# Attention and a rational feed-forward on one core: half-unit sums moved to accumulating DMAs, copies moved from ScalarE to VectorE, all steps reordered

## The chip, the cores and the metric

The kernel runs on one core of a Trainium2 chip. The metric is the device time of one execution in microseconds (us). The runs of the kernel before took 218.06, 218.3 and 219.33 us; their median is 218.3 us.

The core has a matrix engine (TensorE, PE in the profile, with its weight loads as PEld), VectorE (DVE), ScalarE (ACT), GpSimd (POOL) and SyncE (SP). Each engine runs its own instructions strictly in the order in which they were issued to it; an instruction that waits holds up everything behind it on that engine. Loads and stores are DMAs: here SP and ACT issue plain ones (the profile's queues q1 and q10), and POOL issues those that change the type or add to what lies at the target (queue q0). All of them run on the core's 16 DMA engines.

## What is computed

```python
# gated linear attention: 4 batches, 8 heads, 768 steps, head size 48
f = 1.0 / (1.0 + np.exp(-f_logit))
for t in range(S):
    state = f[:, :, t, :, None] * state + np.einsum('bhd,bhe->bhde', k[:, :, t], v[:, :, t])
    y[:, :, t] = np.einsum('bhd,bhde->bhe', q[:, :, t], state)
# feed-forward with a rational activation: 3072 tokens, 384 -> 2048 -> 384; x is y, tokens by heads
h = x @ w_in
P = a[0] + a[1]*h + a[2]*h**2 + a[3]*h**3
Q = 1.0 + abs(b[0])*abs(h) + abs(b[1])*h**2
out = (P / (Q + 1e-06)) @ w_out
```

## The kernel before

**Units.** The work is cut into 12 units (numbered 0 to 11; unit n is chunk n // 4 of batch n % 4) of 256 tokens. A unit passes through an attention part and a feed-forward part. In the feed-forward part the 2048 hidden columns are 16 blocks of 128; a step that takes "8 16" works on blocks 8 to 15, a half unit of 128 partitions x 2048 elements; quarters have four blocks.

**The order.** Nothing schedules the instructions automatically. A string, `ORDER`, lists 861 steps; the program issues them one by one, so this list fixes the order on each engine and each queue. `@n` names one of four PSUM slots of two banks each; a slot is used again only when the last reader of what it held is done. `ld 2 f >mk.0.1` means that this load may not begin before the step `mk 0 1` is done.

**Steps of the attention part**, with their engine: `ld n f/k/q` loads (SP), `ld n v` load (POOL, with a change of type); `ef`, `ls` exp and log of the gate (ACT); `cs` cumulative sums over time by a triangular matrix (PE); `A` their exp (ACT); `xa` products of q and k with them (DVE); `T` transposes (PE) and `Te` their copy out of PSUM (ACT with `s`, else DVE); `sc` scores (PE), `mk` their mask (DVE); `vm` a copy of parts of v (POOL); `yi`, `yb` the output y (PE); `ye` its scaled copy into the feed-forward's input xT (ACT); `kv`, `si` the new state in PSUM (PE); `ae` a small exp (ACT); `st` the state's scaled copy (DVE).

**Steps of the feed-forward part:** `h` (or its halves `ha`, `hb`) the first product (PE); `hy` its copy to bf16 (ACT); `sq` h squared (DVE; `sa` on ACT); `ab` |h| into the tile z (DVE). Then z + h2 is formed in one of three ways: `u` by two matmuls with the identity, followed by `ln` (ACT); `zd` by a DMA that adds h2 to z in memory, or `zv` by DVE, both followed by `lz` (ACT). `ex` is the exp that makes 1/Q out of that log (ACT). `p1`, `p2`, `pm` form the parts of P (DVE); `ta` (a DMA that adds) or `tv` (DVE) forms their sum, the tile gall; `gm` multiplies it by 1/Q (DVE); `o` is the second product (PE), `oe` its copy out of PSUM, `so` the store (SP, the last on ACT).

**At the start** `cz`, `cu`, `ci`, `cm` make constants, `wi` and `wo` load the two weight matrices in four parts each (POOL), `ab_` loads the coefficients a and b, `fa` works out scales from b (nine tiny DVE instructions), `fr` reads two of them into ACT registers, `fb` scales a, and `dz k` issues k matmuls whose result is not used.

The three ways of a sum, as the code has them:

```python
def zd(n, m0, m1):
    nc.gpsimd.dma_start(out=fl(s["z"], m0, m1), in_=fl(s["h2"], m0, m1), accum_op=ALU.add)
def ta(n, m0, m1):
    nc.gpsimd.dma_start(out=fl(s["g"], m0, m1), in_=fl(s["hy"], m0, m1), accum_op=ALU.add)
def tv(n, m0, m1):
    return nc.vector.tensor_add(fl(s["g"], m0, m1), fl(s["g"], m0, m1), fl(s["hy"], m0, m1))
```

## Time and profile before

| | value |
|---|---|
| median of 3 runs | 218.3 us (218.06 to 219.33) |
| span of the profiled execution | 216.3 us, 2.0 us under that median |
| instructions | 7159 |
| DMA traffic | 42.13 MB in 60910 packets |
| `zd` and `ta` DMAs | 18 and 17 |
| `tv` and `zv` on DVE | 9 and 2 |
| granted TensorE clock | 1.000 |

The span runs from the first to the last instruction that the profile shows. "Busy" is the time in which an engine has an instruction under way; for PE the ends of the matmuls are modelled. A row of the profile by line gives the line of the kernel, engine, operation, the tiles written and read, the count, then busy us and the mean duration of one. Line numbers are those of the kernel before; in the changed kernel they are one to five less.

### The profile page before, as it was taken

To read this page: it belongs to the slowest core of one execution; us is meant where nothing else is said; L and a number is where in the kernel's file an instruction comes from. 1 tells how busy PE (TensorE), PEld (TensorE's weight loads), DVE (VectorE), ACT (ScalarE), POOL (GpSimd) and SP (SyncE) were. 2 spreads that over 40 slices of the span, in tenths; PEclk is the share of its full clock that TensorE was granted. 3 is DMA by queue.
4 is the path that set the end of the run, shared out by engine and by line. 5 is a ranking of instruction groups with operands and counts; after the bars stand their busy time and mean duration, and the time that the engine had idled before them with its cause. 6 is when DMAs were issued, how large, how long until landed. Compare 5 with 4: busy or idle time off the path is not lost.

```text
span 216.3 us, 7159 instructions
## 1 busy us (share of the span) xinstructions
PE 203.2 (94%) x3166; PEld 140.1 (65%) x3166; DVE 202.7 (94%) x246; ACT 200.8 (93%) x211; POOL 81.6 (38%) x91
## 2 busy tenths in 40 slices
PE   6989989699799999999999999999999999999993
PEld 2457658468377657658758658668668678676551
DVE  3588999999999999999999999999999999999991
ACT  4746899999999999999999999999999999999991
POOL 5250247120157803014954205954232516433300
PEclk9999999999999999999999999999999999999999
DMA  5999999999598999958999997999889793999863
GB/s 132 248 226 194 243 212 226 207 221 250 136 246 143 231 237 271 149 101 195 197 232 216 211 251 179 173 234 222 160 159 228 142 162 70 170 194 188 154 234 145
DMA packets 60910, 42.13 MB, mean 195 GB/s; under 512 B 51152, under 2 KB 54992, under 8 KB 60880
## 3 DMA queue, kind: packets, MB, share of 16 engines
q0 software_dynamic: 21232, 22.81, 66.0%
q1 hardware_dynamic: 39360, 18.68, 33.7%
q8 instruction: 24, 0.39, 0.7%
q10 hardware_dynamic: 288, 0.20, 0.3%
q14 instruction: 6, 0.05, 0.1%
HBM read 25.17 MB, written 4.72 MB: 138 GB/s over the span
## 4 chain that ended last, share of the span: by engine, by line
ACT 42%; DVE 21%; PE 18%; DMA 8%; issue 6%; POOL 3%; POOLq 0%; ACTq 0%; DVEq 0%
ACT qi L530 11%; ACT hy L488 10%; PE op L570 9%; ACT lq L526 8%; DMA fn<-in_f_logit_dram 4%; DMA z<-h 4%; PE warm L302 3%; DVE gall L548 3%; ACT A L309 3%; DVE scm L360 3%; DVE qkp L315 3%; PE hp L458 2%; DVE gall L560 2%; DVE gall L556 2%; ACT qkT L337 2%
## 5 line engine op out<-in xcount | busy, mean ns | idle before, releaser
L570 PE MATMUL op<-w_out_sb,gall 128*128 128x384 bf16 x384 | 70.1, 326 | 0.4 <-ACT hy L488 0.4
L458 PE MATMUL hp<-xT,w_in_sb 128*128 128x256 bf16 x564 | 65.3, 272 | 1.3 <-ACT xT L439 1.1
L458 PEld LDWEIGHTS <-w_in_sb 128*128 128x128 bf16 x564 | 55.0, 98 | 11.0 <-issue 2.8
L570 PEld LDWEIGHTS <-gall 128*128 128x128 bf16 x384 | 35.5, 98 | 23.6 <-DVE gall L560 0.9
L488 ACT CAST hy<-hp 128x1024 bf16<-128x1024 f32 x48 | 47.4, 1073 | 1.7 <-PE hp L482 1.2
L530 ACT ACTIVATE qi<-lq 128x2048 bf16<-128x2048 f32 (+1 forms) x26 | 46.9, 1845 | 0.0
L367 POOL COPY vmp<-vn 128x128 bf16<-128x128 bf16 x24 | 33.7, 1417 | 32.1 <-DMA vn<-in_v_dram 18.9
L526 ACT ACTIVATE lq<-z 128x2048 f32<-128x2048 bf16 (+1 forms) x20 | 36.9, 1846 | 0.6 <-DMA z<-h 0.5
L552 POOL DMA_DIRECT2D gall<-hy x17 | 14.8, 926 | 50.7 <-ACT A L309 11.5
L522 POOL DMA_DIRECT2D z<-h x18 | 17.3, 1065 | 36.3 <-issue 10.5
L560 DVE TENSOR_TENSOR gall<-gall,qi 128x2048 bf16<-128x2048 bf16 (+1 forms) x26 | 29.6, 1143 | 0.3 <-ACT qi L530 0.2
L548 DVE TENSOR_TENSOR gall<-gall,h 128x2048 bf16<-128x2048 bf16 (+1 forms) x26 | 29.4, 1138 | 0.0
L492 DVE TENSOR_TENSOR h<-hy 128x2048 bf16<-128x2048 bf16 (+1 forms) x26 | 27.3, 1059 | 1.5 <-ACT hy L488 1.4
L360 DVE TENSOR_TENSOR scm<-sc,mask 128x1024 bf16<-128x1024 f32 x24 | 28.4, 1211 | 0.0
L309 ACT ACTIVATE A<-cs 128x768 f32<-128x768 f32 (+1 forms) x26 | 19.6, 816 | 0.0
L500 DVE TENSOR_SCALAR z<-hy 128x2048 uint16<-128x2048 uint16 (+1 forms) x28 | 17.1, 618 | 0.1
L534 DVE TENSOR_SCALAR gall<-hy,a_sb 128x4096 bf16<-128x4096 bf16 (+1 forms) x14 | 16.9, 1210 | 0.2 <-ACT hy L488 0.2
L539 DVE TENSOR_SCALAR hy<-hy,a_sb 128x4096 bf16<-128x4096 bf16 (+1 forms) x14 | 16.6, 1184 | 0.0
L200 POOL DMA_DIRECT2D vn<-in_v_dram x12 | 13.2, 1104 | 2.2 <-PE y L374 2.2
L315 DVE TENSOR_TENSOR qkp<-kn,A 128x768 bf16<-128x768 f32 (+1 forms) x13 | 11.5, 887 | 2.0 <-ACT A L309 2.0
L278 ACT ACTIVATE fn<-fn 128x768 f32<-128x768 f32 (+1 forms) x13 | 10.7, 825 | 2.8 <-DMA fn<-in_f_logit_dram 2.7
L337 ACT COPY qkT<-tp 128x1024 f32<-128x1024 f32 (+1 forms) x12 | 12.5, 1041 | 0.7 <-PE tp L327 0.7
(72 smaller groups left out, 262.2 us busy)
## 6 DMA issues: line engine op xcount, KB each, us to landing
gall<-hy POOLq DMA_DIRECT2D x16, 512.0 KB, 6.7
z<-h POOLq DMA_DIRECT2D x15, 512.0 KB, 7.4
fn<-in_f_logit_dram SPq DMA_DIRECT2D x11, 384.0 KB, 7.4
kn<-in_k_dram SPq DMA_DIRECT2D x11, 384.0 KB, 9.8
qn<-in_q_dram SPq DMA_DIRECT2D x11, 384.0 KB, 7.2
out_dram<-osb SPq DMA_DIRECT2D x11, 384.0 KB, 4.1
vn<-in_v_dram POOLq DMA_DIRECT2D x12, 192.0 KB, 8.0
w_in_sb<-in_moe_w_in_dram POOLq DMA_DIRECT2D x4, 384.0 KB, 8.2
```

Of the source, the lines that this page charges most:

```text
L309: nc.scalar.activation(t, src, AF.Exp, scale=1.0 if x else -1.0)
L315: return nc.vector.tensor_mul(s["qk"][:, :, x, hh, 0:D], s["qk"[x]][:, hh].rearrange("p h i d -> p i h d"), A_sb[:, :, x].rearrange("p i ( ...
L360: return nc.vector.tensor_mul(t, s["sc", g].rearrange("s r a i t -> s (r a) (i t)"), mb)
L367: nc.gpsimd.tensor_copy(s["vm"][:, :, :, 32 * x:32 * x + 16], src)
L458: nc.tensor.matmul(t[:, m - m0, :], w_in_sb[:, kk, m * P:(m + 1) * P], s["x"][:, kk].rearrange("p i j t -> p (i j t)"), start=(kk == 0), s ...
L488: nc.scalar.copy(fl(big(s, "hy", "hy", 3), m0, m1), fl(s["hp", m0], 0, m1 - m0))
L492: return nc.vector.tensor_mul(fl(big(s, "h2", "h2", 2), m0, m1), fl(s["hy"], m0, m1), fl(s["hy"], m0, m1))
L526: nc.scalar.activation(fl(lq, m0, m1), fl(s["z"], m0, m1), AF.Ln, scale=regs[2], bias=1.0 + 1e-6)
L530: nc.scalar.activation(fl(qi, m0, m1), fl(lq, m0, m1), AF.Exp, scale=-1.0)
L548: return nc.vector.tensor_mul(fl(s["g"], m0, m1), fl(s["g"], m0, m1), fl(s["h2"], m0, m1))
L560: return nc.vector.tensor_mul(fl(s["g"], m0, m1), fl(s["g"], m0, m1), fl(qi, m0, m1))
L570: nc.tensor.matmul(s["op", j][:, j, 0:DM], s["g"][:, m, P * j:P * j + P], w_out_sb[:, m, :], start=(s["on", j] == 1), stop=(s["on", j] == KF))
```

## The change

Two step functions get a choice of engine (`hy` gets one too, which the new order does not use):

```diff
     def ye(n, *args):
-        k0, k1 = [x for x in args if x != "s"] or (0, KD)
+        k0, k1 = [x for x in args if x not in ("s", "v")] or (0, KD)
...
-        return nc.scalar.mul(s["x"][:, k0:k1].rearrange("p k i j t -> p j (k i) t"),
-                             s["y"][:, :, k0 * C:k1 * C].rearrange("p j (k t) -> p j k t", t=R), regs[0])
+        dst = s["x"][:, k0:k1].rearrange("p k i j t -> p j (k i) t")
+        src = s["y"][:, :, k0 * C:k1 * C].rearrange("p j (k t) -> p j k t", t=R)
+        if "v" in args:
+            return nc.vector.tensor_scalar(dst, src, sig[:, 0:1], None, op0=ALU.mult)
+        return nc.scalar.mul(dst, src, regs[0])
```

In the list of steps, which has 861 entries again, these differ in kind:

- `ye` of units 2, 3 and 6 goes from ACT to DVE, and so does `Te` of unit 5.
- `tv` becomes `ta` for the halves 0 0 8, 1 0 8, 1 8 16, 2 8 16, 3 8 16 and the quarters 11 8 12 and 11 12 16; `ta 11 0 4` becomes `tv`. That is 23 accumulating DMAs on gall where there were 17, and 3 sums on DVE where there were 9.
- `zd 3 8 16`, `zd 5 8 16` and `zd 11 0 4` become `zv`; `zv 4 8 16` and `zv 6 0 8` become `zd`. That is 17 and 3 where there were 18 and 2.

Every other step stands in the list as often as before, with the same blocks; their places and slots are all new. The start, before:

```
ld 0 f 2 4; cz 0; ab_ b a; cu 0; cz 1; ld 0 f 0 2; ld 1 f; ci; cu 1; ld 0 v; ld 0 k 0 2; ld 0 k 2 4; fa
ld 0 q 2 4; ef 0 2 4; ls 0 2 4; cm; ef 0 0 2; dz 9 @2; cs 0 2 4 @2; fr; cz 3; ls 0 0 2; ld 0 q 0 2; ab_ a s
ld 1 k; dz 5 @3; cs 0 0 2 @3; ef 1; ld 1 q; ls 1; vm 0 1; A 0 1 0 2; wi 12 16 >ls.1; dz 4 @0; cs 1 @0
A 0 1 2 4; xa 0 1 0 2; A 0 0 2 4; wi 8 12; cz 2; A 0 0 0 2; xa 0 1 2 4; dz 3 @1; kv 0 @2; wi 4 8
xa 0 0 0 2; si 0 0; ae 0; dz 1 @1; T 0 0 2 @1; wi 0 4; xa 0 0 2 4; st 0 0; Te 0 0 2 s; T 0 2 4 @3; A 1 1
ld 1 v; Te 0 2 4; A 1 0; vm 0 0; sc 0 0 @1; si 0 1; mk 0 0; sc 0 1 @3; mk 0 1; ld 2 f >mk.0.1; ld 2 k
ld 3 f; yi 0 1 @0; yb 0 0 2; ye 0 0 1 s; xa 1 1; dz 2 @1; yb 0 2 4; ye 0 1 3 s; st 0 1; dz 1 @3
ha 0 12 16 @3; hb 0 12 16; xa 1 0; fb; hy 0 12 16; h 0 8 12 @1; sq 0 12 16; T 1 @3; hy 0 8 12; ab 0 12 16
u 0 12 16 @2; Te 1 s; sq 0 8 12; h 0 4 8 @1; p1 0 8 16; ln 0 12 16; ld 4 f; ab 0 8 12; pm 0 8 16
u 0 8 12 @2; hy 0 4 8; p2 0 8 16; ln 0 8 12; dz 1 @3; sc 1 1 @1; sc 1 0 @3; sq 0 4 8; h 0 0 4 @0; ef 2
```

and in the changed kernel:

```
ld 0 f 2 4; cu 0; cz 1; ld 0 f 0 2; cz 0; ld 1 f; cu 1; dz 5 @3; ld 0 k 2 4; ld 0 q 2 4; ld 0 v; cm; ld 0 q 0 2
dz 9 @0; ld 0 k 0 2; cz 2; ci; ld 1 k; ld 1 q; ef 0 2 4; ab_ a s; ab_ b a; ef 0 0 2; ls 0 0 2; ls 0 2 4
cs 0 0 2 @3; ef 1; cs 0 2 4 @1; ls 1; fa; A 0 0 0 2; vm 0 0; A 0 0 2 4; ld 1 v; A 0 1 0 2; A 0 1 2 4; dz 1 @3
wi 4 8; fr; xa 0 0 2 4; dz 4 @1; xa 0 1 2 4; wi 12 16 >ls.1; xa 0 0 0 2; T 0 2 4 @1; wi 8 12; xa 0 1 0 2
cs 1 @2; Te 0 2 4; T 0 0 2 @3; A 1 1; cz 3; kv 0 @1; A 1 0; xa 1 1; sc 0 1 @0; si 0 0; ae 0; Te 0 0 2 s; mk 0 1
vm 1 1; sc 0 0 @3; vm 0 1; wi 0 4; mk 0 0; yb 0 2 4 @2; ld 2 f >mk.0.1; ld 2 v; ld 3 f; kv 1 @0; ld 2 q; st 0 0
yb 0 0 2; ld 2 k; ae 1; vm 1 0; xa 1 0; yi 0 1; ld 3 k; si 0 1; ld 3 q; ye 0 0 1 s; si 1 0; ye 0 1 3 s; st 1 0
ld 4 k; T 1 @3; ld 4 f; fb; si 1 1; st 0 1; h 0 4 8 @2; Te 1 s; st 1 1; ha 0 12 16 @1; hy 0 4 8; sc 1 0 @0
sc 1 1 @3; mk 1 0; hb 0 12 16; ef 2; dz 1 @2; mk 1 1; hy 0 12 16; h 0 8 12 @2; sq 0 4 8; ls 2; ab 0 12 16
yb 1 0 2 @0; hy 0 8 12; ab 0 4 8; ld 5 f; yb 1 2 4; sq 0 12 16; ld 4 q; yi 1 1; ye 1 s; p1 0 8 16; cs 2 @2; ef 3
h 0 0 4 @3; ...
```

The place of the sum of unit 1's second half, in the changed kernel:

```
sq 2 0 8; h 3 12 16 @1; Te 4 s; gm 0 8 16; h 3 8 12 @2; ls 5; hy 3 12 16; p2 1 0 16; cs 5 @0; hy 3 8 12
sc 4 1 @3; p1 2 0 16; ta 1 8 16; u 1 12 16 @1; A 5 1; ta 1 0 8; A 5 0; h 3 0 4 @2; mk 4 1; vm 5 1; ln 1 12 16
gm 0 0 8; sc 4 0 @3; hy 3 0 4; kv 4 @0; h 3 4 8 @1; p2 2 0 16; ef 6; ex 1 8 16; o 0 1 4 8 @2; pm 2 8 16
o 0 0 0 4; mk 4 0; o 0 1 12 16; ta 2 8 16; ae 4; ls 6; si 4 0; o 0 0 12 16; hy 3 4 8; st 4 0; o 0 0 4 8
gm 1 8 16; ...
```

The end, before and in the changed kernel, from the last block of unit 11's first product on:

```
h 11 12 16 @0
...
o 9 0 4 8 @3; ...; oe 9 0 2 s; ...; so 9 0 2 s; ...; so 7 0 2 s; ...; so 8 0 2 s; ...
oe 10 0 2 s; so 10 0 2 s; o 11 1 8 12; o 11 0 12 16; oe 11 0 1 v; so 11 0 1 s; o 11 1 12 16; oe 11 1 2 s
so 11 1 2 a
```

```
h 11 0 4 @1
...
o 9 1 0 4 @2; ...; o 8 1 0 4; ...; o 8 0 8 12; ...; o 8 0 0 4; ...; oe 8 0 2 s; ...; so 8 0 2 s; ...
so 7 0 2 s; ...; so 6 0 2 s; ...; oe 10 0 2 s; o 11 0 4 8; gm 11 12 16; o 11 1 4 8; so 10 0 2 s
oe 9 0 2 s; o 11 0 12 16; so 9 0 2 s; o 11 1 12 16; oe 11 0 1 v; so 11 0 1 s; oe 11 1 2 s; so 11 1 2 a
```

More of the change, by code (lines that the diff above doesn't have):

```diff
@@ new lines @@
+ta 10 8 16; o 9 0 4 8; hy 11 0 4; o 8 1 0 4; ab 11 4 8; ab 11 12 16; o 8 0 8 12; ex 10 0 8; ab 11 8 12
+sq 11 8 12; o 9 1 4 8; sq 11 0 4; o 8 0 0 4; zd 11 8 12; sq 11 4 8; lz 10 8 16; o 9 0 12 16; zd 11 12 16
+ab 11 0 4; u 11 4 8 @1; p1 11 8 16; gm 10 0 8; o 9 0 8 12; ex 10 8 16; o 9 1 12 16; pm 11 8 12; o 10 0 0 4 @3
+zv 11 0 4; o 10 1 4 8; ln 11 4 8; p2 11 8 16; o 10 0 4 8; p1 11 0 8; lz 11 0 4; ta 11 8 12; o 10 1 0 4
+gm 10 8 16; o 9 1 8 12; lz 11 8 12; o 9 0 0 4; pm 11 12 16; o 10 0 12 16; ex 11 8 12; pm 11 0 4; ta 11 12 16
@@ L105 @@
+o 10 1 12 16; p2 11 0 8; oe 8 0 2 s; o 10 0 8 12; gm 11 8 12; ex 11 0 4; so 8 0 2 s; o 10 1 8 12; tv 11 0 4
+so 7 0 2 s; o 11 0 8 12 @1; lz 11 12 16; so 6 0 2 s; pm 11 4 8; o 11 1 8 12 @0; gm 11 0 4; ex 11 4 8; tv 11 4 8
+o 11 0 0 4; ex 11 12 16; gm 11 4 8; o 11 1 0 4; oe 10 0 2 s; o 11 0 4 8; gm 11 12 16; o 11 1 4 8; so 10 0 2 s
+oe 9 0 2 s; o 11 0 12 16; so 9 0 2 s; o 11 1 12 16; oe 11 0 1 v; so 11 0 1 s; oe 11 1 2 s; so 11 1 2 a
 """
@@ L484, in hk, with hy @@
                              start=(kk == 0 and (m - m0) % 2 == 0), stop=(kk == KD - 1), skip_group_check=True)
-    def hy(n, m0, m1):
+    def hy(n, m0, m1, eng="s"):
         s = unit(n)
-        nc.scalar.copy(fl(big(s, "hy", "hy", 3), m0, m1), fl(s["hp", m0], 0, m1 - m0))
+        (nc.scalar.copy if eng == "s" else nc.vector.tensor_copy)(
+            fl(big(s, "hy", "hy", 3), m0, m1), fl(s["hp", m0], 0, m1 - m0))
     def sq(n, m0, m1):
```

142 lines of the change are left out of this document (57 added, 85 removed).

## Prediction

> **What bounds the kernel now.** I read the page's busy times first, then the stages, then the chain that ended last.
>
> ```profile
> span 216.3 us, 7159 instructions
> PE 203.2 (94%) x3166; PEld 140.1 (65%) x3166; DVE 202.7 (94%) x246; ACT 200.8 (93%) x211; POOL 81.6 (38%) x91
> ...
> 0.00:20.00 20.00, 17.20 (x235) 9.65 (x236) 12.59 (x41) 10.84 (x19) 7.75 (x20) 1.00 1.09 200
> 20.00:30.00 10.00, 9.37 (x190) 6.30 (x187) 9.50 (x15) 9.34 (x12) 2.23 (x4) 1.00 1.29 233
> 30.00:190.50 160.50, 154.42 (x2597) 110.02 (x2598) 159.56 (x162) 159.46 (x162) 66.56 (x61) 1.00 1.02 194
> 190.50:212.83 22.33, 22.25 (x148) 14.13 (x147) 21.06 (x31) 20.70 (x19) 5.09 (x6) 1.00 0.84 189
> ```
>
> The stage rows give length, then busy time of PE, weight loads, DVE, ACT and POOL, then clock, DMA share and GB/s. From 30 to 190.5 us DVE is idle for 160.50 - 159.56 = 0.94 us, ACT for 1.04, PE for 6.08. Three engines are level, so no one of them can be relieved alone to much effect. Idle time lies at the start: by 30 us ACT has lost 30 - 20.18 = 9.8 us, DVE 7.9, PE 3.4. Whatever a new order does there is paid in full, because nothing later has room to make it good.
>
> ```profile
> 6.67 1.09 PE warm L302 x5
> ...
> 16.06 9.14 DMA fn<-in_f_logit_dram
> 25.22 0.85 ACT fn L278
> ...
> 38.57 2.26 DVE h L492 x2
> ...
> 84.63 0.92 ACT qkT L337
> 85.55 1.83 ACT hy L488 x2
> ...
> 189.79 0.71 ACT xT L439
> 190.54 5.40 PE hp L458 x48
> 195.94 4.55 PE op L570 x28
> ...
> 201.43 11.38 PE op L570 x68
> ```
>
> The chain (start, us, what) goes through a gate load of unit 2 issued only at 16.06, then DVE, then ACT, and closes on PE. The times in it are what one more instruction costs on a full engine, less than the durations of single instructions, which overlap.
>
> **What is removed and added.** Five half-unit `tv` leave DVE net, plus one quarter that `zv 11 0 4` puts back. The half-unit products `h L492` have the shape of `tv`: 2.26 / 2 = 1.13 us each, 5 x 1.13 = 5.65 us off DVE. ACT loses three `ye` of 0.71 and one `Te` of 0.92: 3 x 0.71 + 0.92 = 3.05 us off ACT. What they cost on DVE the trace does not show at full size:
>
> ```profile
> L339 DVE COPY qkT<-tp 128x1024 bf16<-128x1024 bf16 x1 | 0.7, 691 | 0.7 <-ACT qkT L337 0.7
> L577 DVE COPY osb<-op 128x384 f32<-128x384 f32 x1 | 0.6, 558 | 0.9 <-PE op L570 0.9
> L315 DVE TENSOR_TENSOR qkp<-kn,A 128x768 bf16<-128x768 f32 x11 | 10.4, 946 | 0.0
> ```
>
> `ye` copies 128x768 float32 out of PSUM: at most 2 x 0.558 = 1.12 us, at least the 0.558 of half of it; the 768-wide product at 0.946 is nearest, and I take 0.9. The full `Te` is twice the 0.691 row: 0.7 to 1.38, I take 1.2. That is 3 x 0.9 + 1.2 = 3.9 us onto DVE (2.4 to 4.7). Net: DVE -5.65 + 3.9 = -1.75 us, ACT -3.05 us, PE nothing. With everything else alike the gain is at most the smaller of the two, and PE, which gets none of it, has 6.08 us of idle in the middle to give.
>
> **The start.** The list moves the load of b behind the first exp of unit 0 on ACT's queue, and `fa`, which needs b, ahead of every `xa` on DVE.
>
> ```profile
> 0.84 0.42 ACTq L219 DMA_DIRECT2D b_sb<-in_moe_b_dram  x1
> 4.18 0.17 DVE L254 TENSOR_SCALAR bm<-b_sb 128x2 uint32<-128x2 uint32 x1 [2.27 <-DMA b_sb<-in_moe_b_dram]
> 4.42 0.52 ACT L278 ACTIVATE fn<-fn 128x384 f32<-128x384 f32 x1 [2.33 <-DMA fn<-in_f_logit_dram]
> 5.51 0.16 DVE L262 TENSOR_TENSOR sig<-bm,sig 128x1 f32<-128x1 f32 x1
> 6.20 0.84 DVE L249 MEMSET state<- 128x192 f32 x4
> 9.02 0.56 DVE L315 TENSOR_TENSOR qkp<-kn,A 128x384 bf16<-128x384 f32 x1 [1.98 <-ACT A L309]
> 14.82 1.21 DVE L360 TENSOR_TENSOR scm<-sc,mask 128x1024 bf16<-128x1024 f32 x1
> ```
>
> b now starts at 4.42 + 0.52 = 4.94, lands 4.18 - 0.84 = 3.34 us later at 8.3, and `fa` (4.18 to 5.67, 1.5 us) ends at 9.8, so the first `xa` is 0.8 us later than at 9.02. Queued behind that wait on DVE are all of unit 0's `xa`, its `Te`, `cz 3` and now also `xa 1 1`, before the first mask; who waits are `T` on PE and, through `fr`, ACT's `A 1 1`. By these durations (four `xa` of some 0.5, `Te` 0.69, `cz 3` 0.84, `xa` 0.9, mask 1.2) the mask `mk 0 1` ends at 15.4, which is when `ld 2 f` may go: about 15.5, against 16.06. Unit 0's `ye` follows the second mask, a state and `yi`, and ends near 18.4; before it was 17.3 by the next rows.
>
> ```profile
> 16.67 0.60 ACT L439 ACTIVATE xT<-y 128x512 bf16<-128x512 f32 x1 [0.75 <-PE y L374]
> 18.49 1.01 ACT L488 CAST hy<-hp 128x1024 bf16<-128x1024 f32 x1 [1.23 <-PE hp L482]
> 23.78 1.03 ACT L513 ACTIVATE lq<-u 128x1024 f32<-128x1024 f32 x1
> 25.22 0.84 ACT L278 ACTIVATE fn<-fn 128x768 f32<-128x768 f32 x1 [0.41 <-DMA fn<-in_f_logit_dram]
> q0 software_dynamic: 1377, 1.36, 120.8%
> q1 hardware_dynamic: 32, 0.01, 0.9%
> ```
>
> Before, ACT did three `hy`, `Te 1` and two `ln` between unit 0's `ye` and the exp `ef 2`, and then waited 0.41 us for its data. Now only `Te 1` and one `hy` stand before `ef 2`. Both loads of f take their 9.14 us in a stretch in which the weights fill the engines: the last two rows are the queues' packets, MB and share of 16 engines from 13 to 20 us, POOL's queue and SP's, and almost nothing of SP's moved. Three of the four weight loads still come ahead of it, and `wi 0 4` now comes beside it. I take 9.14 us again: 24.6 (at worst some 2 us more, at best no wait). ACT reaches `ef 2` near 21.3 and stands until then, with every further `hy`, `ls 2` and `ye 1` behind it. What ACT has done by that exp is 2 `hy` and 2 `ln` less than before, 4 x 0.91 = 3.65 us (1.83 / 2; a `ln` has the shape of a `hy`), less some 0.2 for the `ae 1` pulled ahead, and the exp starts 0.6 earlier: a loss of 3.65 - 0.2 - 0.6 = 2.8 us (0 to 4.9). DVE follows: `ab 0 12 16` waits for the `hy` behind that exp, near 26.4, and by then DVE is some 2.6 us of work behind. PE is short of `cs 2` and unit 1's `h` until 27 to 29 us; by 30 us it has done some 2.2 us less, and six `dz` matmuls (1.09 / 5 = 0.22 each) are still to come: 3.5 us. This is the largest term, and it hangs on where the load of f lands.
>
> **The end** I cost at nothing. PE closes the run back to back, 68 `op` matmuls in 11.38 us, and in the changed list 12 more of them are left when unit 11's `h` ends, so gall's last sums by DMA have more cover, not less. Without that cover the two quarter `ta` would show their landing, row below, against 3.8 us of DVE work in between. One store more waits there for SP's turn; a store lands 4.1 us after its issue, by the first row below, and this one while PE still works.
>
> **DMAs.** Six `ta` more and one `zd` less, 5 half units.
>
> ```profile
> out_dram<-osb SPq DMA_DIRECT2D x11, 384.0 KB, 4.1
> q0 software_dynamic: 21232, 22.81, 66.0%
> q1 hardware_dynamic: 39360, 18.68, 33.7%
> gall<-hy POOLq DMA_DIRECT2D x16, 512.0 KB, 6.7
> gall<-hy POOLq DMA_DIRECT2D x1, 256.0 KB, 3.7
> q0 software_dynamic: 501, 1.01, 96.1%
> L552 POOL DMA_DIRECT2D gall<-hy x17 | 14.8, 926 | 50.7 <-ACT A L309 11.5
> ```
>
> The row of 501 packets is from 198 to 204 us, where only such sums run: 1.01 MB in 6 x 0.961 us, 175 GB/s, so 3 us of all 16 engines for a half unit and 15 us for the five. Between the last input of a `ta` and its `gm` I count 8 to 30 us of DVE instructions nearly everywhere, more than 6.7, so they hide. The closest is `ta 1 8 16`: `p1 2`, `mk 4 1`, a `gm`, `p2 2`, `pm`, `mk 4 0` and `st 4 0`, 7.5 us from the end of `p2 1`. On POOL the issues, 926 ns each, are hidden by its idle time (81.6 us busy); a `ta` or `zd` that stands behind a `vm` which waits is late by that wait, and I count up to 16 us of DVE work for one (`ta 7 8 16`), with 9 us left before its `gm`. The Trainium skill speaks against the change here: in "SBUF — State Buffer", on the trap that DVE blocks DMA, descriptors written by GpSimd wait while DVE runs an instruction that takes the port they share. The row of the issues holds whatever there is of that already: 926 ns each, well inside the slack above.
>
> **The sum.** ACT: 216.3 + 2.8 - 3.05 = 216.0. DVE: 216.3 + 2.6 - 1.75 = 217.2. PE: 216.3 + 3.5 = 219.8, less what its 6.08 us of waits shrink; these are waits on ACT and DVE, which stay as full as before, so I give back 1 us. The span is the latest, 218.8 us, and with the 2.0 us between span and median 220.8 us.
>
> **Rivals.** *The start loses nothing* (0.28). If f lands by 21.5 or ACT comes to it later, only the relief is left: DVE -1.75, ACT -3.05, PE's waits shrink by as much, span about 213.8, 215.8 us. For it: the new weight order leaves one load fewer ahead. Against it: SP's queue got nothing while weights were moving. *PE has slack in its busy time* (0.24). The 68 closing `op` matmuls take 167 ns each, but over the kernel
>
> ```profile
> L570 PE MATMUL op<-w_out_sb,gall 128*128 128x384 bf16 x384 | 70.1, 326 | 0.4 <-ACT hy L488 0.4
> ```
>
> it is 70.1 / 384 = 183 ns, so 384 x 16 ns = 6 us of waits hide in these alone. Then PE makes its 3.5 us good, and DVE's 217.2 stands: 219.2 at most, 218 by ACT; I say 218.7 us. "Trainium Kernel Development and Optimization" of the Trainium skill (Performance Expectations) has it so: matmul busy time is a poor measure of how near the limit PE is, since matmuls are pipelined. By that rule PE's term goes and the time is that of this rival; the rows bear it out in part, as weight loads are busy only 65%. *The DMA engines become the bound* (0.12): 66.0 + 33.7 is already nearly 100% of the span, 15 us more needs 107%, and shares go past 100 only while both queues run (1.29 from 20 to 30 us). Once landings pass 8 us, `lz` and `gm` wait in each unit; 4 us on the forecast, 225 us. That the change does not do what it says is excluded by the counts of the list.
>
> **Chances.** The forecast has 0.36. About 1% (2.2 us) is what a measurement of this kernel can tell from no change. Faster by more is the first rival, 0.28; within 1% the second, 0.24; slower the forecast and the DMA bound, 0.48. The range for 8 in 10 reaches from inside the first rival, 214.8, to inside the last, 224.5; for the forecast alone it is 219 to 223, by the bounds of the load's landing.
>
> **What would show it.** Right: ACT idle before unit 2's exp for 2 to 4 us behind its load; the first mask of unit 0 near 15 us; by 30 us 12 us or more of ACT idle; DVE and ACT full from 30 to 190. Wrong: that exp at 22 us without a wait; PE idle of less than 4 us between 30 us and its last matmul; or `gm` and `lz` waiting on DMAs, which would make the third rival.

## The result and the profile after

| | before | after |
|---|---|---|
| median, measured side by side | 218.44 us, 6 runs (217.6 to 220.35) | 230.04 us, 6 runs (227.67 to 231.32) |
| ratio after / before | | 1.0478, 95% interval 1.0412 to 1.0544 |
| span of the profiled execution | 216.3 us | 226.0 us |
| time of the profiled execution | | 227.67 us, the shortest of the six |

The changed kernel is 4.8% slower. The ratio and its interval compare single runs, without the one run after (231.32 us) that fell in a slower state of the chip, so the ratio lies a little below the quotient of the medians. The sign of the forecast is right; 230.0 us lies above its range, which ended at 224.5. The profiled executions differ by 9.7 us, and those 9.7 us are what the traces can explain; the rest up to the 11.6 us of the medians lies in executions that were not profiled.

First the head of the page of the changed kernel, with the stages that answer to those shown of before (length, busy time of PE, weight loads, DVE, ACT and POOL, clock, DMA share, GB/s):

```profile
span 226.0 us, 7169 instructions
PE 205.6 (91%) x3166; PEld 142.7 (63%) x3166; DVE 202.5 (90%) x245; ACT 198.5 (88%) x207; POOL 81.3 (36%) x96
...
0.00:30.00 30.00, 23.18 (x400) 14.63 (x401) 17.21 (x47) 15.28 (x25) 11.05 (x27) 0.89 1.16 205
90.00:110.00 20.00, 16.92 (x360) 12.49 (x359) 17.09 (x19) 17.35 (x19) 7.73 (x9) 1.00 1.21 216
30.00:190.50 160.50, 151.52 (x2535) 108.64 (x2535) 155.99 (x161) 153.08 (x157) 61.03 (x61) 1.00 1.05 200
190.50:226.00 35.50, 30.88 (x234) 19.44 (x231) 29.31 (x39) 30.11 (x27) 9.26 (x10) 0.99 0.82 185
```

DVE was busy for as long as before, so its idle time is the difference. Span less busy time, stretch by stretch:

| DVE idle, us | before | after | change |
|---|---|---|---|
| 0 to 30 us | 7.9 | 12.8 | +4.9 |
| 30 to 190.5 us | 0.9 | 4.5 | +3.6 |
| from 190.5 us to the end | 4.7 | 6.2 | +1.5 |
| DVE's busy time | 202.7 | 202.5 | -0.2 |

Together 9.8 us, which is the difference of the spans to the rounding. Of the middle's 3.6 us, 2.9 lie between 90 and 110 us alone. The same stretch of before was full:

```profile
90.00:110.00 20.00, 19.62 (x313) 13.48 (x312) 19.95 (x21) 20.00 (x20) 10.75 (x9) 1.00 0.86 167
```

**Who waits in the middle.** In the view of waits (engine, line, waited for: us in total, times, longest) of the changed kernel some rows are new or much longer than before:

```profile
DVE state L447 <- PE sv L427: 6.6, 4, 3.2
PE y L369 <- issue: 5.3, 3, 2.2
ACT xT L438 <- PE y L369: 4.1, 4, 3.3
ACT lq L525 <- DMA z<-h: 1.6, 1, 1.6
```

PE stops up to 2.2 us in the middle of a row of like matmuls, and DVE and ACT wait for it. "issue" means that the profile shows nothing it waited for. Before, the longest such wait at the same line was 0.4 us, that of `xT` for `y` 1.1 and that of `lq` for a sum by DMA 0.5. The first of these stops, which lies in the start, in the order of time (start, us, engine, what, in brackets the idle time before it and its releaser):

```profile
8.28 0.17 DVE L249 TENSOR_SCALAR bm<-b_sb 128x2 uint32<-128x2 uint32 x1 [5.01 <-DMA b_sb<-in_moe_b_dram]
...
9.82 0.55 DVE L310 TENSOR_TENSOR qkp<-qn,A 128x384 bf16<-128x384 f32 x1
...
15.74 1.10 SPq L195 DMA_DIRECT2D fn<-in_f_logit_dram  x2
...
17.40 0.28 PE L369 MATMUL y<-scm,vn 64*32 64x128 bf16 x1
19.86 0.28 PE L369 MATMUL y<-scm,vn 64*32 64x128 bf16 x1 [2.19 <-issue]
...
20.64 0.87 ACT L438 ACTIVATE xT<-y 128x256 bf16<-128x256 f32 x2 [3.26 <-PE y L369]
...
25.21 1.01 ACT L486 CAST hy<-hp 128x1024 bf16<-128x1024 f32 x1 [1.06 <-PE hp L456]
...
26.41 0.84 ACT L273 ACTIVATE fn<-fn 128x768 f32<-128x768 f32 x1 [0.19 <-DMA fn<-in_f_logit_dram]
```

PE was in the middle of `yb 0 0 2`, all inputs there, and did nothing from 17.68 to 19.86. The first `hy` of unit 0 comes at 25.21 where it came at 18.49.

What ends such a stop is a row of the page that is easily passed over, the queue of kind "instruction" (packets, MB, share):

```profile
q8 instruction: 24, 0.39, 0.6%
```

24 packets of 0.39 MB / 24 = 16 KB: PE's own instruction stream, some 6,340 instructions, so about 260 to a packet; that a packet holds 256 is what the run with 768 matmuls below shows. Counting PE's instructions in the trace (weight loads, matmuls and the few semaphore instructions between them, without PE's very first) up to each of its four long stops, and taking the packet nearest in time:

```
stop after   PE stopped       packet            PE ran again   the 256 before
instruction  us               us                us             had taken, us
448          17.68            17.50 to 18.48    19.86          3.6
1472         51.02            50.14 to 51.04    52.46          5.0
2752         92.98            91.85 to 92.81    94.09          4.9
3264         105.62           105.04 to 105.98  107.58         3.6
```

All four counts are 192 more than a multiple of 256, each stop ends 1.3 to 1.6 us after a packet is through, and together they last 6.7 us. The kernel before has no stop at such a count. That the packets hold the instructions behind the stop was my reading of this table; the experiments below test it.

What the stops cost DVE in the middle can be read from its waits there:

```profile
55.33 0.56 DVE L447 TENSOR_TENSOR state<-sv,alast 128x384 bf16<-128x384 f32 x1 [0.72 <-PE sv L427]
...
109.45 0.56 DVE L447 TENSOR_TENSOR state<-sv,alast 128x384 bf16<-128x384 f32 x1 [2.31 <-PE sv L427]
```

These two follow the stops at 51.02 and 105.62 and are 3.0 of the 4.5 us that DVE is idle from 30 to 190.5 us. Another 0.6 is a wait for scores at 101.3, and 0.75 at 157.7 is a wait for ACT, which had stood 1.56 us at an `lz` for its sum by DMA. No wait of DVE stands directly behind the stop at 92.98.

**The end.** The last sums by DMA and the last copy on DVE, in the changed kernel and before:

```profile
214.98 0.69 DVE L559 TENSOR_TENSOR gall<-gall,qi 128x1024 bf16<-128x1024 bf16 x1 [0.17 <-DMA gall<-hy]
...
221.09 0.56 DVE L576 COPY osb<-op 128x384 f32<-128x384 f32 x1 [1.56 <-PE op L569]
```

```profile
212.18 0.56 DVE L577 COPY osb<-op 128x384 f32<-128x384 f32 x1 [0.92 <-PE op L570]
```

DVE waits only 0.17 us for a sum by DMA. The end's 1.5 us are 0.64 more of waiting for PE's last matmuls (1.56 against 0.92) and 0.8 more from that copy to the end of the span (226.0 - 221.65 against 216.3 - 212.74), in which the last stores run.

### The profile page after: what moved, and what is told of

Its sections match the earlier page's. It is cut to its first block, busy times and chain, and to the rows that moved or that the text cites. A ratio compares the mean times of both kernels' runs of the same rounds, so it can differ in the third digit from the quotient of the medians.

```text
span 226.0 us, 7169 instructions
## 1 busy us (share of the span) xinstructions
PE 205.6 (91%) x3166; PEld 142.7 (63%) x3166; DVE 202.5 (90%) x245; ACT 198.5 (88%) x207; POOL 81.3 (36%) x96
## 2 busy tenths in 40 slices
DMA packets 61630, 44.76 MB, mean 198 GB/s; under 512 B 51232, under 2 KB 55072, under 8 KB 61600
## 5 line engine op out<-in xcount | busy, mean ns | idle before, releaser
L456 PE MATMUL hp<-xT,w_in_sb 128*128 128x256 bf16 x564 | 67.6, 274 | 2.5 <-issue 1.4
L456 PEld LDWEIGHTS <-w_in_sb 128*128 128x128 bf16 x564 | 54.9, 98 | 12.8 <-issue 3.8
L486 ACT CAST hy<-hp 128x1024 bf16<-128x1024 f32 x48 | 49.3, 1065 | 2.7 <-PE hp L456 1.9
L551 POOL DMA_DIRECT2D gall<-hy x23 | 24.3, 1085 | 52.8 <-DVE gall L547 17.7
L521 POOL DMA_DIRECT2D z<-h x17 | 18.5, 1127 | 49.3 <-DVE z L499 14.9
L362 POOL COPY vmp<-vn 128x128 bf16<-128x128 bf16 x24 | 25.3, 1095 | 25.3 <-DMA vn<-in_v_dram 17.8
L559 DVE TENSOR_TENSOR gall<-gall,qi 128x2048 bf16<-128x2048 bf16 (+1 forms) x26 | 29.5, 1138 | 0.3 <-DMA gall<-hy 0.2
L499 DVE TENSOR_SCALAR z<-hy 128x2048 uint16<-128x2048 uint16 (+1 forms) x28 | 18.1, 657 | 0.7 <-ACT hy L486 0.7
L447 DVE TENSOR_TENSOR state<-sv,alast 128x384 bf16<-128x384 f32 x20 | 11.0, 549 | 6.6 <-PE sv L427 6.6
L195 POOL DMA_DIRECT2D vn<-in_v_dram x12 | 14.0, 1267 | 5.2 <-issue 4.1
L322 PE MATMUL tp<-ident,qkp 128*128 128x128 bf16 x192 | 13.7, 227 | 0.8 <-DVE qkp L310 0.6
L322 PEld LDWEIGHTS <-qkp 128*128 128x128 bf16 x192 | 12.4, 102 | 3.0 <-DVE qkp L310 1.9
```

The lines of the kernel that those rows point to most:

```text
L322: nc.tensor.transpose(t[:, x, i, p, :], s["qk"][:, i, x, 2 * p:2 * p + 2, :].rearrange("t h d -> t (h d)"), ident)
L362: nc.gpsimd.tensor_copy(s["vm"][:, :, :, 32 * x:32 * x + 16], src)
L456: nc.tensor.matmul(t[:, m - m0, :], w_in_sb[:, kk, m * P:(m + 1) * P], s["x"][:, kk].rearrange("p i j t -> p (i j t)"), start=(kk == 0), s ...
L486: (nc.scalar.copy if eng == "s" else nc.vector.tensor_copy)(fl(big(s, "hy", "hy", 3), m0, m1), fl(s["hp", m0], 0, m1 - m0))
L559: return nc.vector.tensor_mul(fl(s["g"], m0, m1), fl(s["g"], m0, m1), fl(qi, m0, m1))
```

## The experiments

Each kernel was timed beside the kernel before (217.98 to 218.52 us in these comparisons). The edits are to the list of steps.

### Where TensorE's instruction blocks begin

`pz k` issues k matmuls of two columns whose result is not used, early, where PE has time. 70 of them are 140 instructions, so every later step lies 140 further on in the blocks of 256.

```diff
+    def pz(k):
+        for i in range(k):
+            nc.tensor.matmul(warm["t"][32 * (i % 4):32 * (i % 4) + 32, 0, 0:2], Ui[0:64, 0:32], Ui[0:64, 0:2],
+                             start=True, stop=True, skip_group_check=True)
 (changed kernel, k = 70, 108 and 128)
-cs 0 0 2 @3; ef 1; cs 0 2 4 @1; ls 1; fa
+cs 0 0 2 @3; ef 1; cs 0 2 4 @1; pz k; ls 1; fa
```

> 70 matmuls of two columns are added on PE behind the second cumulative sum of unit 0, into the unused tile of the warming matmuls. They shift the places at which PE's instruction stream crosses a multiple of 256 by 140 and change nothing else. Theory A (PE runs out of instructions where 256 of them take less than some 6 us): three of the four long gaps on PE (at 17.7, 93 and 105.7 us) go, one of about 1.8 us and some below 1 us stay or appear, so 8.9 us of stall become about 3, PE's clock stays up at the start, and the time falls by 5 to 8 us to 222 to 225. Theory B (the new order's own waits: the load of f, sums by DMA): nothing gets shorter, 230 or one more.

> The same with 108 matmuls, a shift of 216. Theory A: by the trace of the changed kernel this shift gives the worst stalls of all, 11 us where it now has 9, so 230 to 234, though it differs from the run with 70 by 38 tiny matmuls alone. Theory B: 230 to 231. A plain cost or gain of having more matmuls at the start would put the run with 70 between this one and the changed kernel.

> The changed kernel with 128 unused two-column matmuls at the place where the run with 70 had its own. That is 256 instructions, one whole block, so that every later block begins at the same instruction as in the changed kernel. Theory A, block places decide: the long gaps on TensorE come at the same four steps as in the changed kernel (near 18, 51, 93 and 106 us), and the time is that of the changed kernel or a little more, 229 to 232 us. Rival W, the extra matmuls themselves help: 225 to 227.5 us, as with 70.

| k | shift in the block | time, us | ratio to before (95%) | stops of over 0.6 us at block ends |
|---|---|---|---|---|
| 0 | 0 | 230.04 | 1.0478 (1.0412 to 1.0544) | 2.2, 1.4, 1.1, 2.0 |
| 70 | 140 | 226.25 | 1.0316 (1.0228 to 1.0403) | 0.7, 2.2 |
| 108 | 216 | 227.18 | 1.0370 (1.0307 to 1.0433) | 1.7, 1.7, 1.4 |
| 128 | 256 | 229.69 | 1.0496 (1.0452 to 1.0540) | 1.5, 1.2, 2.3, 0.7, 0.7 |

The run with 128 is the control: the same idle matmuls, and the blocks begin where they did. Its stops come at the same four steps, near 18.8, 51.5, 93.2 and 108.6 us (and one at 169), and its time is that of the changed kernel. With 70 the stretch that was emptied most is full:

```profile
90.00:110.00 20.00, 19.52 (x390) 13.95 (x379) 20.00 (x23) 19.32 (x21) 7.78 (x9) 1.00 1.23 218
```

DVE 20.00 of 20, against 17.09. So where the blocks begin costs time by itself: against the control, the shift by 140 takes some 3.4 us off the median, less than the 5 to 8 us that I had expected. It does not take off all: another stop of 2.2 us came at 46 us, and ACT waited 2.9 us for a sum by DMA until 154.9, so the profiled span, 225.1 us, is only 0.9 shorter. The run with 108 was a miss: I had expected it to be the worst, and it was better than the changed kernel. The stops that a shift will give, and what they cost, could not be read off the old trace.

In the kernel before:

```diff
 (first run)
-dz 4 @0; cs 1 @0
+dz 1 @0; pz 36; cs 1 @0
 (second run)
-ld 1 k; dz 5 @3
+ld 1 k; dz 2 @3; pz 26
...
-dz 4 @0; cs 1 @0
+dz 1 @0; pz 52; cs 1 @0
...
-dz 3 @1; kv 0 @2
+dz 1 @1; pz 26; kv 0 @2
```

> The kernel before, with 36 matmuls of two columns in place of three warming matmuls at the start: a shift of 66 instructions. Theory A: by the trace of the kernel before its own places give 0.2 us of stall, and this shift gives 9 us (eight places of up to 2.3 us); some of it is hidden by engines that wait anyway, so 221 to 227. Theory B: the order is untouched, 218 to 219.

> The kernel before, with 104 such matmuls in place of eight warming ones at the start: a shift of 192 instructions. Theory A: this shift gives 0.5 us of stall, so 218 to 219.5, less than with 36. If more matmuls at the start cost time by themselves, it is slower than with 36. Theory B: 218 to 220.

The first was a miss: 218.27 us, ratio 0.9970 (0.9942 to 0.9998), no stop at a block's end, although some blocks of 256 now ran in 3.8 to 5.5 us. Their packets had come earlier, 1.7 to 5.0 us before PE needed them. So a quick block is not enough. That the next packet is asked for in time where PE has work waiting in its queue fits this, but was not tested. The second took 217.66 us, 0.9950 (0.9920 to 0.9979), as expected without stops; half a per cent less than the kernel before is below the 1% that I had called the least that can be told from no change.

To see the supply by itself, one run puts 768 such matmuls, six blocks, in a row:

```diff
 (kernel before)
-ef 0 0 2; dz 9 @2; cs 0 2 4 @2
+ef 0 0 2; dz 9 @2; pz 768; cs 0 2 4 @2
```

> The old kernel with 768 unused matmuls of two columns in a row at its start, before its first cumulative sums: 1536 TensorE instructions, six blocks of 256. In the earlier run 70 of them took 0.5 us, 7 ns each. Theory A, TensorE holds one block ahead and asks for the next only when it enters the last one it has: after the first one or two blocks the row runs in bursts of 128 matmuls with a gap behind each, one burst every 6 us or so, each gap ending 1.1 to 1.6 us behind an instruction packet: five gaps and 20 to 35 us more for the kernel. Rival Q, the queue keeps several blocks in advance: 768 x 7 ns = 5.4 us and no gap over 0.5 us, some 4 us more for the kernel.

246.65 us against 218.52, one execution of each, 28.1 us more. PE in the order of time:

```profile
5.76 1.90 PE L307 MATMUL warm<-Ui 64*32 64x2 bf16 x214
12.41 1.18 PE L307 MATMUL warm<-Ui 64*32 64x2 bf16 x128 [4.76 <-issue]
18.61 1.17 PE L307 MATMUL warm<-Ui 64*32 64x2 bf16 x128 [5.02 <-issue]
24.53 1.18 PE L307 MATMUL warm<-Ui 64*32 64x2 bf16 x128 [4.75 <-issue]
27.98 1.18 PE L307 MATMUL warm<-Ui 64*32 64x2 bf16 x128 [2.28 <-issue]
31.71 0.46 PE L307 MATMUL warm<-Ui 64*32 64x2 bf16 x42 [2.55 <-issue]
```

Bursts of exactly 128 matmuls with their 128 weight loads, and a stop behind each: theory A as it was put. The packets run from 9.70 to 10.93, 16.19 to 17.12, 22.13 to 23.11, 25.65 to 26.61 and 29.18 to 30.34; PE goes on 1.4 to 1.5 us after each. The distance of two bursts is 6.2 and 5.9 us first and then 3.5 and 3.7. The DMA traffic fell at the same time, by the stages of this run:

```profile
6.00:20.00 14.00, 4.00 (x460) 3.77 (x447) 1.18 (x7) 2.21 (x4) 4.48 (x7) 1.00 1.29 222
20.00:32.00 12.00, 2.65 (x297) 2.48 (x297) 0.00 (x0) 0.00 (x0) 1.35 (x3) 1.00 0.52 53
```

With the DMA engines full (share 1.29) the packet starts 3.5 to 3.8 us after the burst before it began; of the two packets that start after 25 us, with the share at 0.52 in that stage, each starts 1.1 to 1.2 us after. So 256 PE instructions without a lead took about 6 us here while the DMA engines were full, however short the matmuls. The four stops of the changed kernel give the same: the 256 instructions and the stop behind them took 5.6 to 6.4 us, with the DMA share at 1.16 by 30 us and 1.05 behind. The Trainium skill describes this queue in "Runtime: NRT & Kernel Launch" (Instruction fetch mechanics): blocks of 16 KiB, 256 instructions, fetched by the sequencer through a DMA queue of its own, which agrees with the 24 packets of 16 KB. It also says that the fetch is hidden because the sequencer dispatches more slowly than the blocks come; the run above shows five stops of 2.3 to 5.0 us.

### The order and the split, each alone

The first run keeps the changed order and puts back all seventeen steps of the split; the second keeps the old order and takes the new split.

```diff
 (changed order, old split)
-ye 2 v; ye 3 v; ye 6 v; Te 5; ta 0 0 8; ta 1 0 8; ta 1 8 16; ta 2 8 16; ta 3 8 16
+ye 2 s; ye 3 s; ye 6 s; Te 5 s; tv 0 0 8; tv 1 0 8; tv 1 8 16; tv 2 8 16; tv 3 8 16
-zv 3 8 16; zd 4 8 16; zv 5 8 16; zd 6 0 8; zv 11 0 4; ta 11 8 12; ta 11 12 16; tv 11 0 4
+zd 3 8 16; zv 4 8 16; zd 5 8 16; zv 6 0 8; zd 11 0 4; tv 11 8 12; tv 11 12 16; ta 11 0 4
 (old order, new split: the same lines the other way round)
```

> The changed kernel's order with all seventeen steps of the split put back as they were (the four copies on ScalarE, the sums by VectorE or DMA as before). Theory A, the order carries the loss: ScalarE is 90% and VectorE 90% of a stretched span, so the 1.75 us of relief on VectorE and 3.05 us on ScalarE that go away are worth little or are lost in full: 229 to 233 us, and the gaps of 1 to 2.5 us on TensorE stay where they are by instruction count (the split moves no TensorE instruction). Rival S, the split carries it (copies out of PSUM on VectorE, more accumulating DMAs): 218 to 222 us.

> The old order with the new split in place of the old one: four copies to VectorE, and each sum made by DMA or VectorE as in the changed kernel, at its old place in the list. Theory A, the order carries the loss: 216 to 219.5 us in the body, plus what the two last quarter sums cost that now stand directly ahead of their product without cover (some 3 us of landing each, partly in parallel with other work): 217 to 223 in all, with the extra shown after 205 us in the trace and the stretch from 30 to 190 no longer than before. Rival S, the split carries the loss: 226 to 231 us, with VectorE or ScalarE waiting on accumulating DMAs in the middle.

Measured: 243.30 us, 1.1140 (1.1098 to 1.1183), and 233.59 us, 1.0672 (1.0611 to 1.0734). Both theories fail. Each half alone is worse than the two together: the new split costs 15 us in the old order and saves 13 in the new one. That is what an order fitted to its split would show. In the waits of the old order with the new split:

```profile
ACT lq L527 <- DMA z<-h: 7.4, 3, 3.8
...
DVE gall L561 <- DMA gall<-hy: 4.6, 3, 2.9
```

Sums by DMA, at places which were chosen for a DVE instruction, come late, 12 us of waiting where the kernel before has 0.5. In the changed order waits for sums by DMA come to 2.6 us (ACT 1.6 at `lz` and 0.8 at a `hy` whose tile a sum still reads, DVE 0.2): there they have more cover. The changed order with the old split waits 10.5 us for them (7.5, 0.9 and 2.1).

### The named parts in the old order

So I gave the sums more cover: each of the five stands directly behind the last step that writes its inputs. The copies alone, and both, are two more runs; a fourth moves the blocks of "both" with 104 matmuls as above.

```diff
 (kernel before; five sums)
-tv 0 0 8; tv 1 0 8; tv 1 8 16; tv 2 8 16; tv 3 8 16      (at their places)
+ta 0 0 8      (behind pm 0 0 8)
+ta 1 8 16; ta 1 0 8      (behind p2 1 0 16)
+ta 2 8 16      (behind pm 2 8 16)
+ta 3 8 16      (behind pm 3 8 16)
 (four copies)
-ye 2 s; ye 3 s; ye 6 s; Te 5 s
+ye 2 v; ye 3 v; ye 6 v; Te 5
```

> The old kernel with five half-unit sums of units 0 to 3 made by accumulating DMAs in place of VectorE, each placed directly behind the last step that writes its inputs (so 17 to 38 steps and more ahead of its product). Theory C, such sums cost nothing where enough VectorE work lies between: VectorE is relieved of 5 x 1.13 = 5.65 us, ScalarE and TensorE, as full as VectorE, are not, so the gain is 0 to 2 us: 216 to 218.5 us. Rival D, 15 us more of DMA engine time is what costs: 220 to 224 us, with VectorE or ScalarE waiting on accumulating DMAs.

> The old kernel with only the four copies (ye of units 2, 3 and 6, Te of unit 5) on VectorE. By the measured durations VectorE gains 3 x 1.01 + 1.21 = 4.2 us of work in a stretch in which it has no idle time, ScalarE loses 3.05 us: 220 to 222.5 us. If VectorE's order absorbs it: 217.5 to 219 us.

> The old kernel with both: the five sums by early DMAs and the four copies on VectorE, so VectorE 5.65 - 4.2 = 1.4 us less and ScalarE 3.05 us less. Theory C, the change's parts are worth this in any order that leaves the sums their cover: 215.5 to 218 us. Rival O, an order that was fitted to the old split loses with any other: 219.5 to 224 us.

> The same, with 104 matmuls of two columns in place of seven of the unused early ones, which move every 16 KB block of TensorE instructions by 192 of 256 and took 0.5% off the old kernel. If block places matter alike in both: 0 to 1.5 us below the run without them; if a block now ends behind dense steps: 1 to 4 us above it, with gaps of over 1 us behind instruction packets.

| | time, us | ratio (95%) |
|---|---|---|
| five sums by early DMA | 225.08 | 1.0312 (1.0266 to 1.0357) |
| four copies on DVE | 221.51 | 1.0133 (1.0092 to 1.0174) |
| both | 225.35 | 1.0303 (1.0257 to 1.0350) |
| both, blocks moved | 225.06 | 1.0310 (1.0270 to 1.0349) |

Theory C is wrong; rival D is right in kind, and the loss is 1 us above its range: 6.6 us lost although DVE has 5 us less to do. The loss stands between 40 and 100 us, where the weights for the second product and the loads of the units are under way as well. That stretch, before and with the five sums, and where DVE, ACT and PE stop in the latter:

```profile
40.00:100.00 60.00, 56.12 (x925) 38.77 (x914) 59.65 (x61) 59.40 (x63) 16.10 (x13) 1.00 1.01 201
```

```profile
40.00:100.00 60.00, 52.10 (x818) 35.76 (x814) 49.10 (x52) 53.81 (x56) 20.34 (x20) 0.97 1.16 228
```

```profile
63.46 1.23 DVE L561 TENSOR_TENSOR gall<-gall,qi 128x2048 bf16<-128x2048 bf16 x1 [3.40 <-DMA gall<-hy]
...
69.05 5.67 POOL L364 COPY vmp<-vn 128x128 bf16<-128x128 bf16 x1
...
74.66 1.71 POOL L523 DMA_DIRECT2D z<-h  x1
...
83.49 1.91 ACT L527 ACTIVATE lq<-z 128x2048 f32<-128x2048 bf16 x1 [4.85 <-DMA z<-h]
...
86.15 2.72 PE L458 MATMUL hp<-xT,w_in_sb 128*128 128x256 bf16 x12 [4.69 <-ACT xT L440]
```

The DMA share rises from 1.01 to 1.16, and two things go wrong. First, a new sum is late for its own product: `ta 1 0 8`, issued at 53.19 right behind `ta 1 8 16`, is there only when DVE has stood 3.40 us at `gm 1 0 8`, 10.3 us after the issue. Some 7.4 us of DVE's work lay between the sum's last input and that product, more than the 6.7 us of the row by which I had called such sums hidden. Second, an older sum is late on another engine's path: POOL is held 5.67 us by a `vm` (3.90 at the same place before), `zd 3 0 8` goes out behind it at 74.66 (70.81 before) and lands when ACT has stood 4.85 us at its `lz`; behind that `lz` on ACT is `ye`, and PE waits 4.69 us for it. How much of the 6.6 us is the first and how much the second was not tested apart. In the run with both parts the first alone goes further, since `ye 3` now stands on DVE behind the late product:

```profile
64.30 1.23 DVE L561 TENSOR_TENSOR gall<-gall,qi 128x2048 bf16<-128x2048 bf16 x1 [4.45 <-DMA gall<-hy]
...
66.50 3.79 PE L458 MATMUL hp<-xT,w_in_sb 128*128 128x256 bf16 x17 [5.15 <-DVE xT L439]
```

The copies alone cost 3.1 us, as expected from their durations, since DVE was full; together with the sums they cost nothing more. Rival O, at 219.5 to 224 us, comes nearest to the 225.35 of both parts. Moving the blocks changes nothing here, and the trace of the run with the sums has no stop at a block's end.

### The start

```diff
 (old list through ln 0 4 8, 118 steps, then the changed list; and the changed list through ye 1 s, 117 steps, then the old list)
```

> The old list through its step ln 0 4 8 (its first 118 steps, about 30 us), then the rest of the changed list in its order and split. Theory H, the start is worth 4.9 us and the rest keeps its loss: 224 to 226.5 us. If the start were everything: 218 to 221 us. If nothing of it counts (rival M): 228 to 231 us. The gaps on TensorE behind instruction packets will fall at other instructions of the body, since the start issues its matmuls in another order; in the stretch from 30 to 200 us I expect one to three of them.

> The changed kernel's list through unit 1's copy into the feed-forward input (its first 117 steps, about 30 us), then the rest of the old list in the old order and with the old split. Theory H, the start costs what VectorE is short by 30 us, 22.08 - 17.21 = 4.9 us: 222 to 225 us. Rival M, the start is made good later because the old body has slack: 217.5 to 220 us. Rival X, moving the start also moves where every later 16 KB block of TensorE instructions begins and opens gaps in the old body: above 225 us, with gaps of 1 to 2.5 us behind instruction packets.

The new start before the old rest takes 227.16 us, 1.0401 (1.0355 to 1.0447): 8.8 us lost, above the expected 222 to 225, and without a new stop in the rest. The stages show 5.3 us of it on DVE by 30 us (16.79 against 22.08) and 3 more where the two lists meet:

```profile
0.00:30.00 30.00, 23.34 (x395) 14.68 (x398) 16.79 (x48) 14.35 (x24) 10.47 (x24) 0.89 1.16 194
30.00:50.00 20.00, 15.94 (x190) 10.90 (x192) 16.95 (x22) 17.06 (x21) 5.93 (x9) 1.00 1.26 229
```

The old start before the new rest, 231.01 us, 1.0558 (1.0513 to 1.0604), gains nothing, which was rival M's number but not for its reason. The start itself is kept and lost again at the join:

```profile
0.00:28.00 28.00, 24.89 (x314) 14.64 (x317) 20.06 (x51) 17.99 (x27) 9.19 (x23) 1.00 1.14 209
28.00:40.00 12.00, 9.44 (x158) 6.94 (x159) 5.30 (x8) 7.39 (x12) 3.78 (x6) 0.72 1.31 230
```

5.30 of 12 us of DVE, where the kernel before has 12.00: unit 1's attention, which the old start leaves for later, is now alone in a row. That is an exchange of two lists that were not made for each other, so it does not price the start. The table of DVE's idle time above says what DVE had lost by 30 us; that none of it is made good later was not tested.

Two runs look inside the new start. In the first unit 0's first quarter of `h` goes ahead of unit 1's `kv`, `si`, `st` and `T`; in the second the load of unit 2's gate is not held until the first mask as well.

```diff
 (changed kernel)
-ld 3 f; kv 1 @0; ld 2 q; st 0 0
+ld 3 f; ld 2 q; st 0 0
...
-ye 0 0 1 s; si 1 0; ye 0 1 3 s; st 1 0
-ld 4 k; T 1 @3; ld 4 f; fb; si 1 1; st 0 1; h 0 4 8 @2; Te 1 s
+ye 0 0 1 s; ye 0 1 3 s; h 0 4 8 @2; kv 1 @0; ae 1
+si 1 0; st 1 0; ld 4 k; T 1 @3; ld 4 f; fb; si 1 1; st 0 1; hy 0 4 8; Te 1 s
 (second run, besides)
-ld 2 f >mk.0.1
+ld 2 f
```

> The changed kernel with one difference in its start: unit 0's first quarter product (h 0 4 8) now stands directly behind ye 0, ahead of unit 1's kv, si, st and T, where it was behind them. Theory W, the start is held by the load of unit 2's gate whatever TensorE does: the first hy comes at 19 to 21 us instead of 25.2, ScalarE then reaches unit 2's exp early, stands 3 us or more behind its load, and the exp begins near 26 us as before; 228.5 to 230.5 us. Rival P, the start is held by TensorE (its stall without instructions and the half clock behind it): the exp begins by 23 us and the time falls to 225 to 227.5 us.

> The same, and the load of unit 2's gate no longer waits for the first mask, so that SP issues it near 10 us instead of 15.7. Theory W: ScalarE no longer waits at unit 2's exp, which begins at 21 to 23 us; by 30 us ScalarE and VectorE are 2 to 4 us ahead of the changed kernel, 225.5 to 228 us, and at least 2 us below the kernel with the held load. Rival P: the two kernels are within 1 us of each other. Rival L: the early load delays q and k of units 0 and 1, the first products come later, and the time does not fall at all (229 us or more).

230.88 us, 1.0587 (1.0553 to 1.0622), and 229.36 us, 1.0478 (1.0408 to 1.0549). The exp of unit 2's gate in the one and in the other, on ACT:

```profile
26.60 0.84 ACT L273 ACTIVATE fn<-fn 128x768 f32<-128x768 f32 x1 [1.83 <-DMA fn<-in_f_logit_dram]
```

```profile
27.24 0.85 ACT L273 ACTIVATE fn<-fn 128x768 f32<-128x768 f32 x1
```

In the first, theory W holds in its mechanism, though the time is 0.4 us above its range: PE no longer stops for instructions there, `hy` comes 3 us earlier (22.29), and the exp begins at 26.60 all the same, now after 1.83 us of waiting for its load. The second is near rival L, and theory W fails: the load is early, issued at 10.92, and the exp is later still, without a wait for it. PE is late instead: the first matmul of `h` waits 1.51 us for the weights until 20.18, and the clock row stands at 0.50 from 16 to 29.5 us (0.87 in the first run), so that unit 1's 16 transposes take 1.91 us where they take 1.05 in the first. Which of the two holds the exp there was not tested.

### The end, and all remedies together

```diff
 (changed list through zd 10 0 8, 755 steps, then the rest of the old list with the old split)
```

> The changed list through its step zd 10 0 8 (755 of 861 steps, about 195 us), then the rest of the old list in the old order and with the old split, so that unit 11's last two quarter sums are again on VectorE. Theory E, the new end costs what VectorE and TensorE wait there for the last sums by DMA (1.5 us of VectorE's idle time after 200 us): 227.5 to 229 us. Rival N, the end is only late because all before it is: 229.5 to 231 us. Rival D, the end is most of the loss: below 226 us.

> The changed kernel with all remedies together: 70 matmuls of two columns early (which move where each 16 KB block of TensorE instructions begins), unit 0's first product earlier, the load of unit 2's gate not held, and the old end. If the pieces add up: 230.0 - 3.8 (measured for the 70 matmuls) - 2 to 4 (start) - 1.5 (end) = 220.5 to 222.5 us. If they overlap, or new places run out of instructions: 223 to 227 us. Below 218 us would mean that the middle of the new order is better than the old one.

The old end: 231.72 us, 1.0642 (1.0578 to 1.0706), more than the changed kernel; theory E fails, which agrees with the 0.17 us above. This join, too, has a stop of its own: DVE stands 1.76 us at 204, where the lists meet. All together: 230.27 us, 1.0578 (1.0522 to 1.0634), no gain either, far from the sum of the parts. In that run DVE is full from 90 to 130 us, but it has done less by 30 us (15.46 us of work, with the clock at one half from 17.4 to 27.7 us), stands 2.26 us near 156 behind ACT, which had waited 3.0 us for a sum by DMA, and 2.04 us at 203, where the old end is joined. I found no version of the new order that reaches the kernel before.

## Why the prediction was wrong

**The parts of the sum.** The counts and most prices were right. What went from DVE and came to it, in the rows of the changed kernel and of the kernel before:

```profile
L437 DVE TENSOR_SCALAR xT<-y,sig 128x768 bf16<-128x768 f32 x3 | 3.0, 1008 | 0.0
...
L334 DVE COPY qkT<-tp 128x2048 bf16<-128x2048 bf16 x1 | 1.2, 1209 | 0.0
```

```profile
L556 DVE TENSOR_TENSOR gall<-gall,hy 128x2048 bf16<-128x2048 bf16 x6 | 7.3, 1211 | 0.0
```

A `ye` took 1.01 us where I had 0.9, the `Te` 1.21 where I had 1.2, a half `tv` 1.21 where I had 1.13. The planned change of DVE's work was -1.75 us; its busy time fell by only 0.2, because other instructions ran longer (the `ab` rows, 17.1 to 18.1 us, are the largest part). ACT's fell by 2.3, forecast 3.05. PE's rose by 2.4, forecast nothing; a part of that is the half clock at the start (16 transposes 1.91 us, at full clock 1.06), the rest was not traced.

**The start, steps.** The chain to the mask came out: `fa` ended at 9.8, the load of f went at 15.74 (15.5 forecast). It then took some 10.5 us (until 26.2), not 9.14. The wait of 2 to 4 us on ACT before unit 2's exp did not show, 0.19 us, because PE had stopped and ACT came late by itself; the run with `h` first showed that a wait of 1.83 us stands right behind. **The start, size.** 2.6 us on DVE forecast, 4.9 measured, 2.8 on ACT forecast and 4.9 measured (14.7 us idle by 30 us against 9.8), which is the upper bound I gave for ACT. The term was right in its place and half its size.

**The step that failed.** It is the one that took everything behind the start as unchanged: PE's waits, the prediction says, "are waits on ACT and DVE, which stay as full as before", and among its signs stands "DVE and ACT full from 30 to 190". The sum for PE, which gave the forecast, takes 1 us off for that stretch; the one for DVE, "216.3 + 2.6 - 1.75 = 217.2", has no term for it. I took it for full because it had been full, but it was full by an order, and that order was gone. In its place PE's idle time there grew from 6.08 to 8.98 us, and DVE lost 3.6 us; 3.0 us of DVE's waits stand behind two of PE's stops for instructions, at 51 and 105 us. With 2.3 us more at the start, 1.55 us of relief that did not come and the end's 1.5, that is 8.95 us on the 217.2 forecast for DVE: the span of 226.0 is there to 0.2 us. For PE the 3.5 us forecast for the start came out at 3.4 (26.57 us done by 30 us before, 23.18 after); the rest of the 9.7 us between the spans is made up by 2.9 us more of idle time in the middle, 2.4 more of busy time and 1.1 more of idle time at the end, where the prediction had minus 1, nothing and nothing. No step of the prediction asked how fast PE gets its instructions, though the row of that queue stands on the page before, too.

**The end.** "The end I cost at nothing" was right about the sums by DMA, which kept their cover (0.17 us of waiting); DVE lost 1.5 us there all the same, behind PE's last matmuls and in the last stores. The run with the old end does not price it, since it stops at its join.

**The rivals.** That the DMA engines become the bound was put at 4 us and 0.12. In the changed kernel the engines waited 2.6 us for sums by DMA in all, so it did not decide; in the old order, with five of the same sums and 6.6 us lost, such waits are what the trace shows. The step "they hide" held for each sum's own product in the changed order (0.17 us), but not in the old one, where one landed 10.3 us after its issue; and it looked at nothing else that POOL issues. The remark that shares go past 100% only while both queues run was wrong on the rows shown: from 13 to 20 us POOL's queue alone stands at 120.8%, SP's at 0.9%. That the start loses nothing is excluded by DVE's 4.9 us; its price of 215.8 us did not follow either, since with 1.75 us off DVE its own sum gives a span of 214.55 us, not 213.8. That PE has slack would have shown as less than 4 us of idle time of PE from 30 us on; it was idle for 8.98 us by 190.5.

**What stays open.** How much of the 11.6 us the instruction stops make: the control and the run with 70 matmuls differ by 1.0496 against 1.0316, but by moving blocks new stops and a late sum came up, so 3.4 us is what one shift was worth, not the whole. Of the 4.9 us at the start little was won back: no version of the new start that I ran had more than 17.59 us of DVE's work done by 30 us (22.08 before). Whether the stops would be shorter with less DMA traffic (the change moves 44.76 MB, before 42.13) was not tested in this kernel. When the sequencer asks for the next packet was not settled either; the old kernel with 36 matmuls shows only that quick blocks need not stop PE.
